# The first phase of an attention and maxout kernel written as one table, with the short group last and group 1 cut into a 4-tile chunk and three of 512 columns

## The chip, the cores and the metric

The kernel runs on one core of a Trainium2 chip. The metric is the time of one execution on the device in microseconds. The engines are named as in the profile: PE is the matrix engine (PEld its weight loads), DVE the vector engine, ACT the scalar engine, POOL the GpSimd engine, and SP (SyncE) the engine that issues nearly all transfers; SPq is SP's queue of transfer issues.

## The reference

For four batches of 12544 tokens with 128 channels, 32 inducing points first attend to all tokens, then every token attends to the 32 states that come out; each result goes through a maxout layer with an output projection.

```python
def mab(q, kv):
    s = scale * (q @ kv.transpose(0, 2, 1))
    s = s - s.max(-1, keepdims=True)
    a = np.exp(s)
    a /= a.sum(-1, keepdims=True) + 1e-09
    return a @ kv
h = mab(I, x)                       # 32 states for each batch
attn = mab(x, h)                    # tokens look at the states
y = np.maximum(np.maximum(attn @ w1, attn @ w2), attn @ w3) @ w_out
```

x is (4, 12544, 128); w1, w2 and w3 are (128, 768) and w_out is (768, 128). The weights arrive as 64-bit numbers.

## The kernel before

**Groups, chunks, slots.** The 98 tiles of 128 tokens of a batch form seven groups: group 0, the short one, has two tiles, groups 1 to 6 have sixteen. A full group makes four chunks of 512 columns, the short one a chunk of 256. A chunk is six slots, one for each 128 of the 768 hidden columns, so there are 600 slots in all. PE does two products for each slot (`pu`, L683, and `pv`, L689) out of the attention weights `pT` of the chunk and the batch's matrix `us` (states times weights, in a high and a low part). ACT takes the positive part of `pu` (L698), DVE the larger of both (`h`, L716), ACT makes the high part (`hi`, L705) and POOL, sometimes DVE, the low part (`lo`). `stage2` then adds three products for each slot into the chunk's output (L741 to L743, one more at its start, L740), six slots behind. `finish` copies the output and sends it off.

**First phase (batch 0).** Only batches 1 to 3 come with a transposed copy of x. For batch 0 PE transposes each group (`transpose_x`, L275) and ACT copies the result to `xT`. Then comes, group by group, the softmax of the 32 queries over the tokens: `attend_products` (PE, L285), `attend_max` (DVE), `attend_column` (ACT), `attend_spread` (PE, L309), `attend_least` (DVE), `attend_weights` (ACT), `attend_transpose` (DVE), `attend_sums` (PE, L360), `attend_keep` (ACT). The `combine_...` functions join the groups into the states `hT` (L528). Meanwhile the four weights are turned from 64 bits to float32 in the steps of `convert` (letters t, T, p, z, r, A or a, d, S), mostly on DVE. `transpose_w2` and `prep_products` form w2 times w_out, `prep_out` the high and low parts of w_out.

**From hT to the pipeline.** `scores_products` (PE, L599) and the ten steps of `scores_steps` give the token softmax of a group; its high and low part are `ph` and `pl`. For a full group `probs` copies four quarters of each chunk's rows into `pT` by transfers on SP (L668); the short group has its weights transposed on PE instead. `first_products` and `first_high`, `first_low` make `us`.

**What sets the order.** The schedule is manual: each engine runs its instructions in the order in which the program writes them, and SP issues its transfers in that order. `LOADS` orders the first loads (0 to 6 are groups, 7 w2, 8 w_out, 9 w1, 10 w3). `phase1_first` writes the first phase as a loop over the groups with the conversion steps of `WORK` in between; `ORDER` is a string for the stretch from hT to the pipeline, in which `d` puts two filler products on PE (`keep_busy`, L410). From then on `main` goes slot by slot: `advance` writes the products of the next slot, then come `probs` for the chunk two ahead (at the fifth slot of each chunk), `finish`, what `plan` holds for the slot, and `stage2`. `plan` spreads the scores of the next group and the first attention of the next batch (`softmax1`: maximum and `exchange_maxima`, six transfers on SP, L321, then `running_least` on DVE, L325) over the slots. The buffers that matter: five of `xg` (a group's tokens), one for the short group's, seven of `xT`, four of `pT`.

Of the kernel before, what the change touches and what calls it, by code (L numbers as in the profile page):

```python
# [25 lines left out]
def kernel(ctx, tc, x, xt, ind_t, w1, w2, w3, w_out, out):  # L26
# [4 lines left out]
    P = 128  # L31
# [7 lines left out]
    LOADS = (0, 1, 2, 7, 3, 8, 4, 5, 9, 6, 10)  # L39

    WORK = (
        "",
        ("0t 0T 0p 0z", "0r 0A"),
        ("1t 1T 1p 1z", "1r 1A"),
        ("0d 1d", "2t"),
        ("2T 2p 2z", "2r 2A"),
        ("3t 3T 3z", "3p 2d 2S"),
        "3r",
        "3a 3d 3S",
    )  # L50


    ORDER = "a a a a b a a b 0 c d m b a b a b a p d b 1 c s b b b s S m b q 2 c s 3 c s d s s d s"
# [70 lines left out]
    raws = []  # L124
    def first_loads():
        for what in LOADS:
            if what < NG:
                xg_next[(0, what)] = load_group(0, what, pieces=4 if what == 1 else 1)
            else:
                raws.append(load_raw(srcs[what - NG]))  # L130
# [79 lines left out]
    w2t = []  # L210

    def transpose_w2():
        for h in range(2):
            tpw = bank_v[h]
            for k in range(3):
                j = 3 * h + k
                nc.tensor.transpose(out=tpw[:, k * P : (k + 1) * P], in_=wf[:, 0, j * P : (j + 1) * P], identity=ident)
            w2h = hp.tile([P, 512], F32, name="w2h", tag="ru", bufs=3)
            nc.scalar.copy(out=w2h[:, : 3 * P], in_=tpw[:, : 3 * P])
            w2t.extend(w2h[:, k * P : (k + 1) * P] for k in range(3))  # L220

    def prep_products():

        wo = wf[:, 1, :].rearrange("p (j c) -> p j c", c=C)
        pw = bank_u[1]
        for j in range(NJ):
            nc.tensor.matmul(out=pw[:, :C], lhsT=w2t[j], rhs=wo[:, j, :], start=(j == 0), stop=(j == NJ - 1))

    def keep_products():
        nc.scalar.copy(out=wcat[:, 2 * DF :], in_=bank_u[1][:, :C])  # L230

    def prep_out():
        wo = wf[:, 1, :].rearrange("p (j c) -> p j c", c=C)
        nc.scalar.copy(out=wo_hi, in_=wo)
        nc.gpsimd.tensor_sub(out=wo_lo, in0=wo, in1=wo_hi.bitcast(F32))

# [3 lines left out]
    def start_batch(b):  # L240
        st = state[b] = {"xT": {}, "xg": {}, "a": {}, "s": {}}
# [28 lines left out]
    def transpose_x(b, gi, k):  # L270
        st = state[b]
        n = min(4, groups[gi]["nt"] - k)
        tps = (bank_u + bank_v)[k // 4]
        for i in range(n):
            nc.tensor.transpose(out=tps[:, i * P : (i + 1) * P], in_=st["xg"][gi][:, k + i, :], identity=ident)  # L275
        xv4 = st["xT"][gi].rearrange("p (q t l) -> p t q l", q=NQ, l=M)
        nc.scalar.copy(out=xv4[:, k : k + n, :, :], in_=tps[:, : n * P].rearrange("p (t q l) -> p t q l", q=NQ, l=M))  # L277
# [12 lines left out]
    def attend_max(b, gi):  # L290

        w = groups[gi]["nt"] * M
        st = state[b]
        mq = wk.tile([P, 1], F32, name="mq", tag="mq") if b == 0 else st["mx"][:, gi, 0:1]
        nc.vector.tensor_reduce(out=mq, in_=st["a"][gi][:, :w], axis=AX.X, op=ALU.max, negate=True)
        st["mq"] = mq

    def attend_column(b):

        st = state[b]  # L300
        md = wk.tile([P, NQ], F32, name="md", tag="md")
        nc.scalar.mul(out=md, in_=quad, mul=st["mq"])
        st["md"] = md

    def attend_spread(b, bank=None):

        st = state[b]
        st["mp"] = bank or spare[0]
        nc.tensor.matmul(out=st["mp"][:, :NQ], lhsT=sel, rhs=st["md"], start=True, stop=True)  # L309
# [102 lines left out]
    def phase1_first():  # L412

        start_batch(0)
        nc.sync.dma_start(out=iT, in_=ind_t)
        nc.scalar.mul(out=iT, in_=iT, mul=scale)
        first_loads()
        def half(gi, k):
            if gi < NG:
                if k == 0:  # L420
                    start_group(0, gi)
                for i in (k, k + 4):
                    transpose_x(0, gi, i)

        start_group(0, 0)
        keep_busy(6, bank_o[1])
        transpose_x(0, 0, 0)
        keep_busy(2, bank_o[1])
        attend_products(0, 0, bank_a[0])
        attend_max(0, 0)  # L430
        attend_column(0)
        half(1, 0)
        attend_spread(0, bank_o[0])
        attend_least(0, 0)
        half(1, 8)
        work(WORK[0])
        st = state[0]
        for gi in range(NG - 1):
            last = gi == NG - 2
            attend_products(0, gi + 1, bank_a[(gi + 1) % 2])  # L440
            attend_weights(0, gi)
            half(gi + 2, 0)
            attend_max(0, gi + 1)
            attend_column(0)
            half(gi + 2, 8)
            if gi > 0:
                attend_sums(0, gi - 1, bank_o[1])
                attend_keep(0, gi - 1)
            attend_transpose(0, gi)
            if not last:  # L450
                work(WORK[gi + 1][0])
            attend_spread(0, bank_o[0])
            attend_least(0, gi + 1)
            if gi == 3:
                transpose_w2()
            if last:
                prep_products()
            else:
                work(WORK[gi + 1][1])
        combine_least(st)  # L460
        work(WORK[NG - 1])
        combine_weights(st)
        attend_weights(0, NG - 1)
        keep_products()
        attend_sums(0, NG - 2, bank_o[1])
        attend_keep(0, NG - 2)
        combine_mask(st)
        combine_groups(st, range(NG - 1), bank_u[0])
        attend_transpose(0, NG - 1)
        sum_groups(st)  # L470
        attend_sums(0, NG - 1, bank_o[1])
        total_sums(st, bank_o[0])
        attend_keep(0, NG - 1)
        work(WORK[NG])
        invert_total(st)
        combine_groups(st, range(NG - 1, NG))
        combine_states(st, NQ)

# [19 lines left out]
    def combine_groups(st, which, bank=None):  # L498
        if which[0] == 0:
            st["sum"] = bank  # L500
        for gi in which:
# [4 lines left out]
                start=(gi == 0),  # L506
                stop=(gi == NG - 1),
# [28 lines left out]
    def first_products(st, which, bank):  # L536
        if which == 0:
            st["us"] = bp.tile([P, UW], F32R, name="us", tag="us")
            st["up"] = {}
# [3 lines left out]
        st["up"][which] = up, st["us"][:, cs]  # L543

# [456 lines left out]
```

## Time and profile before

| | us |
|---|---|
| median of 3 runs | 819.2 |
| lowest, highest | 818.54, 819.29 |
| the profiled execution | 818.58 |
| its span | 816.8 |
| PE busy in the span | 804.4 |
| ACT busy | 740.4 |
| POOL busy | 651.0 |
| DVE busy | 624.8 |

The span runs from the first to the last instruction; the execution's time has 1.8 us around it. Matmuls are pipelined, so PE's busy time says where it does nothing, and the distance from start to start says what a group of matmuls costs. In rows of the timeline come the start, the duration of the group, the engine, the line, the operation, what it writes and reads, the shapes, how many there are, and in brackets the idle time before and what ended it. A product in float32 shows as two records, a float32 transpose as one.

### The profile page before, as it was taken

The page shows a single profiled execution, that of the slowest core. Times are in us where ns is not written, and L with a number is a line of the kernel's source. Part 1 is how long each engine was busy: PE and PEld are TensorE (multiplying, and loading weights), DVE is VectorE, ACT ScalarE, POOL GpSimd, SP SyncE. Part 2 cuts the span into 40 slices and gives each one's busy share as a digit, 9 for nine tenths or more (in the row PEclk, how much of TensorE's full clock was granted, in tenths as well). Part 3 has the DMA queues.
Part 4 walks back from the last instruction along what each step waited for, and adds up shares of the span by engine and source line. Part 5 has one row for each costly group of instructions (what it writes and reads, how often), then busy time and mean ns, then how long its engine had stood idle before and what let it go on. Part 6 is the DMA issues. An engine that isn't in the chain of part 4 may idle for free.

```text
span 816.8 us, 14868 instructions
## 1 busy us (share of the span) xinstructions
PE 804.4 (98%) x4562; PEld 628.4 (77%) x4562; DVE 624.8 (76%) x1072; ACT 740.4 (91%) x1537; POOL 651.0 (80%) x521
## 2 busy tenths in 40 slices
PE   7989999999999999999999999999999999999998
PEld 5757778777788787777778777877878788787886
DVE  4978778777787687787786877877778788778874
ACT  5779889899899898898999988989889899899996
POOL 1369779878799798787888977977879889888887
PEclk9999999999999999999999999999999999999999
DMA  8843645263444453443534354523232222222221
GB/s 329 310 142 98 187 131 173 84 200 107 144 136 123 114 192 89 151 155 112 174 107 135 98 166 145 171 81 105 55 86 78 72 77 78 66 83 75 62 78 52
DMA packets 54287, 102.55 MB, mean 126 GB/s; under 512 B 19648, under 2 KB 23616, under 8 KB 48960
## 3 DMA queue, kind: packets, MB, share of 16 engines
q1 hardware_dynamic: 54064, 101.48, 39.4%
q8 instruction: 36, 0.59, 0.3%
q14 instruction: 43, 0.35, 0.1%
q10 hardware_dynamic: 144, 0.13, 0.0%
HBM read 48.12 MB, written 25.69 MB: 90 GB/s over the span
## 4 chain that ended last, share of the span: by engine, by line
PE 94%; DMA 3%; ACT 1%; DVE 1%; SPq 1%; issue 0%; DVEq 0%
PE acc L741 17%; PE pu L683 16%; PE pv L689 16%; PE acc L742 16%; PE acc L743 16%; PE aux L599 3%; PE acc L740 3%; PE acc L360 3%; PE aux L285 2%; DMA xg<-in_x_dram 2%; DMA pT<-pl 1%; ACT ru L698 0%; PE pu L275 0%; SPq L100 0%; ACT hi L705 0%; PE pv L275 0%
## 5 line engine op out<-in xcount | busy, mean ns | idle before, releaser
L713 POOL TENSOR_TENSOR lo<-h,hi 128x512 fp32r<-128x512 f32 (+1 forms) x502 | 635.8, 1298 | 124.9 <-ACT hi L705 83.1
L716 DVE TENSOR_TENSOR h<-pv,ru 128x512 f32<-128x512 f32 (+1 forms) x600 | 403.6, 675 | 165.1 <-PE pv L689 79.3
L698 ACT ACTIVATE ru<-pu 128x512 f32<-128x512 f32 (+1 forms) x600 | 376.2, 627 | 51.1 <-PE pu L683 48.0
L705 ACT CAST hi<-h 128x512 fp32r<-128x512 f32 (+1 forms) x600 | 387.2, 645 | 0.6 <-DVE h L716 0.3
L741 PE MATMUL acc<-hi,wo_hi 128*128 128x512 f32 (+1 forms) x600 | 235.1, 392 | 0.0
L683 PE MATMUL pu<-pT,us 128*128 128x512 f32 (+1 forms) x600 | 232.1, 387 | 0.5 <-DMA pT<-pl 0.4
L689 PE MATMUL pv<-pT,us 128*128 128x512 f32 (+1 forms) x600 | 232.0, 387 | 0.3 <-DVE h L716 0.3
L742 PE MATMUL acc<-hi,wo_lo 128*128 128x512 f32 (+1 forms) x600 | 231.3, 386 | 0.0
L743 PE MATMUL acc<-lo,wo_hi 128*128 128x512 f32 (+1 forms) x600 | 231.2, 385 | 0.0
L741 PEld LDWEIGHTS acc<-hi,wo_hi 128*128 128x128 f32 x600 | 112.6, 188 | 30.8 <-issue 8.7
L683 PEld LDWEIGHTS pu<-pT,us 128*128 128x128 f32 x600 | 112.6, 188 | 25.7 <-ACT ru L698 2.0
L689 PEld LDWEIGHTS pv<-pT,us 128*128 128x128 f32 x600 | 112.6, 188 | 23.8 <-DVE h L716 1.6
L743 PEld LDWEIGHTS acc<-lo,wo_hi 128*128 128x128 f32 x600 | 112.7, 188 | 23.1
L742 PEld LDWEIGHTS acc<-hi,wo_lo 128*128 128x128 f32 x600 | 112.7, 188 | 21.8
L719 DVE TENSOR_TENSOR lo<-h,hi 128x512 fp32r<-128x512 f32 x98 | 70.9, 724 | 1.5 <-ACT hi L705 1.5
L758 ACT COPY o<-acc 128x512 f32<-128x512 f32 (+1 forms) x99 | 61.2, 618 | 0.0
L740 PE MATMUL acc<-pT,us 128*128 128x512 f32 (+1 forms) x100 | 38.8, 388 | 0.0
L360 PEld LDWEIGHTS acc<-xg,aT 128*32 128x32 f32 x768 | 21.1, 110 | 11.3 <-issue 6.9
L285 PE MATMUL aux<-xT,iT 128*32 128x512 f32 x192 | 25.3, 598 | 1.6 <-ACT xT L277 1.6
L360 PE MATMUL acc<-xg,aT 128*32 128x128 f32 x768 | 25.6, 274 | 0.0
L599 PE MATMUL aux<-xT,hT 128*32 128x512 f32 x192 | 25.1, 603 | 0.0
L192 POOL TENSOR_TENSOR rest<-rest,t 128x768 f32<-128x768 f32 x3 | 5.5, 1827 | 23.9 <-DVE rest L184 23.9
(121 smaller groups left out, 422.0 us busy)
## 6 DMA issues: line engine op xcount, KB each, us to landing
out_dram<-o SPq DMA_DIRECT2D x95, 256.0 KB, 2.1
xg<-in_x_dram SPq DMA_DIRECT2D x23, 1024.0 KB, 6.1
xT<-in_xt_dram SPq DMA_DIRECT2D x18, 1024.0 KB, 5.6
pT<-ph SPq DMA_DIRECT2D x192, 64.0 KB, 2.0
pT<-pl SPq DMA_DIRECT2D x192, 64.0 KB, 2.0
raw<-in_w_dram SPq DMA_DIRECT2D x3, 768.0 KB, 8.9
us<-uh SPq DMA_DIRECT2D x24, 52.0 KB, 1.9
us<-ul SPq DMA_DIRECT2D x24, 52.0 KB, 1.9
```

What stands on the lines that cost most here:

```text
L360: nc.tensor.matmul(out=hps[q * M : (q + 1) * M, :C], lhsT=aT[:, t * M : (t + 1) * M], rhs=xg[:, t, :], start=(t < NQ), stop=(t + NQ >= nt),)
L683: nc.tensor.matmul(out=pu[:, :w], lhsT=state[c.b]["us"][:, 2 * j * P : (2 * j + 1) * P], rhs=c.pT[:, :w], start=True, stop=True)
L689: nc.tensor.matmul(out=pv[:, : d.w], lhsT=state[d.b]["us"][:, (2 * j + 1) * P : (2 * j + 2) * P], rhs=d.pT[:, : d.w], start=True, stop=True,)
L698: nc.scalar.activation(out=ru[:, :w], in_=pu[:, :w], func=AF.Relu)
L705: nc.scalar.copy(out=hi[:, : c.w], in_=h[:, : c.w])
L713: nc.gpsimd.tensor_sub(**args)
L716: nc.vector.tensor_max(out=h[:, : d.w], in0=pv[:, : d.w], in1=relus.pop(s)[:, : d.w])
L719: nc.vector.tensor_sub(**low)
L740: nc.tensor.matmul(out=c.acc[:, :w], lhsT=us[:, 2 * DF :], rhs=c.pT[:, :w], start=True, stop=False)
L741: nc.tensor.matmul(out=c.acc[:, :w], lhsT=wo_hi[:, j, :], rhs=c.hh[j][:, :w], start=False, stop=False)
L742: nc.tensor.matmul(out=c.acc[:, :w], lhsT=wo_lo[:, j, :], rhs=c.hh[j][:, :w], start=False, stop=False)
L743: nc.tensor.matmul(out=c.acc[:, :w], lhsT=wo_hi[:, j, :], rhs=c.hl[j][:, :w], start=False, stop=(j == NJ - 1))
```

## The change

- One table, `FIRST`, is the order of everything from the start to slot 12; `WORK`, `ORDER` and `phase1_first` are gone. A letter is a function and the digits are its arguments (T transposes, C copies, P products, M maximum, D, R, N, E, X, S, K the further steps of the first attention; B and Q filler products; U, h, l, g, H the making of `us`; y `probs` of a chunk; z `stage2`).
- `LOADS` begins with groups 1, 2 and 3, the short group and w_out come last; group 1 comes in two pieces instead of four; `iT` is loaded on ACT's queue. The groups are joined in the order of `TURN`.
- The fillers are seven at the start (before six and two) and 19 single ones (before four pairs).
- Group 1 of batch 0 is cut into a chunk of its first four tiles (`HEAD`), whose weights are transposed on PE, and three chunks of 512 columns over the other twelve tiles, whose rows are 384 columns long (`pieces`). Its softmax runs as two (steps `a` and `b`).
- The scores of group 2 move from the head to slot 12; batch 1's group 0 moves: its maximum from slot 10 to 13, `running_least` from slot 16 to 18, the next load of tokens from slot 7 to 13. `stage2` runs four slots behind until slot 13, then six.
- `prep_products` and the rest of w_out move behind hT; the addition of w3 goes from DVE to POOL; of chunk 1, slots 1 and 4 have their low parts on DVE.

```diff
-    LOADS = (0, 1, 2, 7, 3, 8, 4, 5, 9, 6, 10)
...
+    LOADS = (1, 2, 3, 7, 4, 9, 5, 10, 6, 0, 8)
+    TURN = (1, 2, 3, 4, 5, 6, 0)
+    HEAD = 4
+    LOWHEAD = (1, 4)
+    FIRST = (
+        "B7 T11 T10 T13 C11 T12 C10 C13 C12 P1 M1 D1 T22 C22 T23 T21 R1 T20 C23 N1 E1 X1 T33 T32 C20 T30 C21 "
+        "C33 0t 0T T31 0z 0p S1 0r C30 C31 P2 C32 K1 T41 P3 C41 M2 M3 D2 0A B1 R2 T42 N2 2t D3 R3 T43 E2 T40 "
+        "C42 B1 C43 B1 T52 0d 2T T51 N3 T53 C40 C52 X2 C51 2p T50 C53 P4 C50 3t S2 2r E3 P5 3z B1 3T T60 3p "
+        "M4 T63 2z K2 D4 C60 B1 R4 M5 X3 T61 N4 D5 C63 3r T62 T00 1t R5 C61 E4 W1 C62 N5 2A B1 1T S3 X4 E5 "
+        "C00 P6 K3 P0 X5 M6 S4 1z B1 D6 M0 R6 2d n2 B1 K4 N6 3A D0 B1 R0 1p S5 E6 N0 W0 E0 cl X6 K5 S6 2S cw "
+        "X0 lw lt K6 cm w1 S0 3d K0 1r cg123456 3S cg0 iv B1 hT B1 qS sT qA qB aT U1 w0 sm U0 am sx se bT 1A "
+        "sr ax ae g1 si bm sp bx h1 B1 h0 su sh 1d be sl ar B1 Oh br U2 ai l0 ap bi js bp h2 Gp au ks g2 bu "
+        "H1 Ol H2 Gk s0 ah Q1 s1 bt U3 al n3 4h s2 Q1 Q1 bh Q1 Q1 s3 ja ka 4l bl y2 s4 y3 Q1 s5 z0 s6 z1 s7 "
+        "z2 s8 z3 z4 s9 z5 s10 y4 s11 z6 s12 z7 "
     )
-    ORDER = "a a a a b a a b 0 c d m b a b a b a p d b 1 c s b b b s S m b q 2 c s 3 c s d s s d s"
+    STEPS1 = (7, 8, 9, 10, 11, 11, 12, 13, 14, 15)
     STEPS2 = (3, 5, 7, 8, 9, 10, 11, 13, 14, 15)
...
-                xg_next[(0, what)] = load_group(0, what, pieces=4 if what == 1 else 1)
+                xg_next[(0, what)] = load_group(0, what, pieces=2 if what == LOADS[0] else 1)
...
-        nc.sync.dma_start(out=iT, in_=ind_t)
+        nc.scalar.dma_start(out=iT, in_=ind_t)
...
+    def probs(c):
+
         if c.q is None:
+            probs_transposes(c, bank_a[1])
+            probs_keep(c, nc.vector.tensor_copy)
+            return
+        src = state[c.b]["p", c.gi, c.first]
+        c.pT = pT = wk.tile([P, 512], F32R, name="pT", tag="pT", bufs=4)
+        for r in (0, 2, 1, 3):
+            for q, at, n, to in c.pieces:
+                nc.sync.dma_start(
+                    out=pT.bitcast(F32)[r * M : (r + 1) * M, to : to + n], in_=src[r % 2][q * M : (q + 1) * M, at : at + n]
                 )
...
+    def pieces(k):
+
+        row = (GT - HEAD) * M
+        ends = sorted({512 * k, 512 * k + 512} | {q * row for q in range(NQ) if 0 < q * row - 512 * k < 512})
+        return [(a // row, a % row, b - a, a - 512 * k) for a, b in zip(ends, ends[1:])]
...
+            kinds = [(None,)]
+            if groups[gi]["nt"] == GT:
+                kinds = [(q,) for q in range(NQ)]
+                if b == 0 and gi == 1:
+                    kinds = [(None, HEAD)] + [(k + 1, None, pieces(k)) for k in range(NQ - 1)]
...
-                elif b > 0 or g > 1:
+                else:
                     first.append((scores_products, b, g + 1, bank_a[0]))
-                softmax2(b, g + 1, *(s0 + i for i in STEPS2))
+                softmax2(b, g + 1, *(s0 + i for i in (STEPS2 if b > 0 or g > 1 else STEPS1)))
...
-                        at(s0 + 1, load_tokens, 1, 4)
+                        at(s0 + 7, load_tokens, 1, 4)
...
-                    softmax1(n, 0, s0 + 2)
+                    softmax1(n, 0, *((s0 + 2,) if b > 0 else (s0 + 5, -1)))
...
-            burst(s0 + 2, *first)
+            burst(s0 + 2 if b > 0 or g > 1 else s0 + 6, *first)
...
-            if s >= LAG:
-                c, j = slots[s - LAG]
-                stage2(c, j)
-                if j == NJ - 1:
-                    over = c
+            if done[0] <= s - (LAG if s >= begins[0] + 8 else LAG - 2):
+                over = second()
...
+            "B": lambda n: keep_busy(n, bank_u[1]),
+            "Q": lambda n: keep_busy(n, bank_o[0]),
...
+            "qS": lambda: scores_products(0, 0, bank_u[0]),
+            "qA": lambda: scores_products(0, 1, bank_a[0], 0, HEAD),
+            "qB": lambda: scores_products(0, 1, bank_a[1], HEAD),
+            "js": lambda: probs_transposes(first, bank_u[1]),
+            "ks": lambda: probs_keep(first, nc.scalar.copy),
+            "ja": lambda: probs_transposes(head, bank_a[0]),
+            "ka": lambda: probs_keep(head, nc.scalar.copy),
+            "n2": lambda: (start_batch(1), load_channels(1, 0)),
+            "n3": lambda: load_channels(1, 1),
```

In the table, lower-case pairs that begin with s, a or b are steps of the softmax of the short group, of the head and of the twelve other tiles (`bh` and `bl` are the high and low part of the last, `ph` and `pl`), s with a number is an `advance`, z with a number a `stage2`.

More of the change, by code (lines that the diff above doesn't have):

```diff
@@ L268, in load_channels, with transpose_x, keep_x @@
         state[b]["xg"][gi] = xg_next.pop((b, gi))
[L270 to L277, printed above, removed]
+    def transpose_x(gi, i):
+        st = state[0]
+        if gi not in st["xT"]:
+            start_group(0, gi)
+        tps = (bank_u + bank_v)[i]
+        for k in range(min(4, groups[gi]["nt"])):
+            nc.tensor.transpose(out=tps[:, k * P : (k + 1) * P], in_=st["xg"][gi][:, 4 * i + k, :], identity=ident)
+    def keep_x(gi, i):
+        n = min(4, groups[gi]["nt"])
+        tps = (bank_u + bank_v)[i]
+        xv4 = state[0]["xT"][gi].rearrange("p (q t l) -> p t q l", q=NQ, l=M)
+        nc.scalar.copy(
+            out=xv4[:, 4 * i : 4 * i + n, :, :], in_=tps[:, : n * P].rearrange("p (t q l) -> p t q l", q=NQ, l=M)
+        )
     def attend_products(b, gi, bank):
@@ L410, in keep_busy, with begin @@
             nc.tensor.matmul(out=bank[:, 2 * P : 3 * P], lhsT=ident, rhs=ident, start=True, stop=True)
-    def phase1_first():
+    def begin():
         start_batch(0)
-        nc.sync.dma_start(out=iT, in_=ind_t)
+        nc.scalar.dma_start(out=iT, in_=ind_t)
         nc.scalar.mul(out=iT, in_=iT, mul=scale)
         first_loads()
[L418 to L477, printed above, removed]
     def combine_least(st):
@@ L745, in finish @@
     def finish(c):
[L746 removed]
+        g = groups[c.gi]
+        at = g["at"] + (c.q or 0) * c.w
         o = op.tile([P, 512], F32, name="o", tag="o", bufs=3)
+        if c.q is None and c.last < g["nt"]:
+            nc.scalar.copy(
+                out=o.rearrange("p (q t l) -> p t q l", q=NQ, l=M), in_=c.acc.rearrange("p (t q l) -> p t q l", q=NQ, l=M)
+            )
+            nc.sync.dma_start(
+                out=out[c.b, :, at : at + g["nt"] * P].rearrange("p (q n) -> p q n", q=NQ)[:, :, : c.w // NQ],
+                in_=o.rearrange("p (q n) -> p q n", q=NQ),
+            )
+            return
+        if c.first:
+            nc.scalar.copy(out=o, in_=c.acc)
+            for q, col, n, to in c.pieces:
+                col += g["at"] + (q * g["nt"] + HEAD) * M
+                nc.sync.dma_start(out=out[c.b, :, col : col + n], in_=o[:, to : to + n])
+            return
         if c.n == len(chunks) - 1:
@@ L779 @@
     plan = [[] for _ in range(len(slots) + LAG)]
-    per_batch = nch * NJ
-    short = NJ if groups[0]["nt"] < GT else 0
+    begins = [min(c.n for c in chunks if c.b == b and c.gi == 1) * NJ for b in range(B)]
     WIN = NQ * NJ
@@ L881, with second, main @@
                         at(s0 + 18, load_channels, n + 1, 1)
-            burst(s0 + 2, *first)
+            burst(s0 + 2 if b > 0 or g > 1 else s0 + 6, *first)
             burst(s0 + 15, *second)
-    def main():
-        over = None
-        for s in range(len(slots) + LAG + 1):
+    done = [0]
+    def second():
+        c, j = slots[done[0]]
+        done[0] += 1
+        stage2(c, j)
+        return c if j == NJ - 1 else None
+    def main(start, over):
+        for s in range(start, len(slots) + LAG + 1):
             if s >= LAG:
@@ new lines @@
+        for step in FIRST.split():
+            kind, rest = step[0], step[1:]
+            if step in names:
+                names[step]()
+            elif kind in steps and not rest.isdigit():
+                next(steps[kind])
+            elif kind == "c":
+                combine_groups(st, [int(g) for g in rest[1:]], bank_u[0])
+            elif kind.isdigit():
+                convert(int(kind), rest)
+            elif kind == "s":
+                advance()
+            elif kind == "z":
+                if over:
+                    finish(over)
+                over = second()
+            elif kind == "f":
+                finish(over)
+                over = None
+            elif kind == "y":
+                probs(tails[rest])
+            else:
+                one[kind](*[int(v) for v in rest])
@@ L947 @@
+        for gen in steps.values():
+            assert next(gen, None) is None
+        main(pipe["next"], over)
 _GT = 16
```

270 lines of the change are left out of this document (138 added, 132 removed).

## The prediction

> **What bounds the kernel now.** The page first: TensorE is busy 98% of the span, and the granted clock reads full everywhere. Then the busy time by stages, which says where the missing 2% lie.
>
> ```profile
> PE 804.4 (98%) x4562; PEld 628.4 (77%) x4562; DVE 624.8 (76%) x1072; ACT 740.4 (91%) x1537; POOL 651.0 (80%) x521
> PEclk9999999999999999999999999999999999999999
> ```
> ```profile
> 1.30:20.20 18.90, 14.74 (x108) 10.40 (x108) 8.69 (x20) 11.25 (x25) 2.34 (x3) 1.00 0.94 352
> 20.20:41.90 21.70, 20.41 (x306) 15.73 (x306) 19.53 (x34) 15.39 (x39) 7.35 (x5) 1.00 0.79 296
> 41.90:53.90 12.00, 10.17 (x62) 5.53 (x62) 9.67 (x24) 8.02 (x21) 6.46 (x7) 1.00 0.35 114
> 53.90:71.00 17.10, 17.10 (x90) 13.94 (x90) 14.23 (x26) 16.54 (x37) 15.88 (x14) 1.00 0.58 177
> 71.00:800.00 729.00, 728.89 (x3942) 572.28 (x3941) 564.79 (x958) 678.50 (x1397) 607.54 (x482) 1.00 0.38 116
> ```
>
> The columns after the window are its length and then the busy time of PE, weight loads, DVE, ACT and POOL. From 53.9 us on PE stands still for 0.1 us in 746. So whatever the change does to the time shows as an earlier or later arrival at one given PE instruction of the full pipeline, with the same work done by then. I use the `pv` product of slot 21 (at 70.91, below): before it, both kernels have run the first phase, all weight products, the scores of group 2, the attention product of batch 1's group 0 and the output products of slots 0 to 14. In the first 53.9 us PE idles 4.2 + 1.3 + 1.8 us plus 1.3 us of start, and runs 16 filler products (the first eight below, in 16 records; the others by four `d` of ORDER).
>
> ```profile
> 1.37 2.93 PE L410 MATMUL acc<-ident 128*128 128x128 f32 x12 [1.37 <-POOL ident masks.py:199]
> ...
> 4.51 0.65 PE L410 MATMUL acc<-ident 128*128 128x128 f32 x4
> ...
> 20.24 1.09 PE L275 MATMUL pu<-ident,xg 128*128 128x128 f32 x8 [0.73 <-DMA xg<-in_x_dram]
> 21.17 1.04 PE L275 MATMUL pv<-ident,xg 128*128 128x128 f32 x8
> 22.13 1.08 PE L360 MATMUL acc<-xg,aT 128*32 128x128 f32 x32
> 23.14 0.39 PE L309 MATMUL acc<-md,sel 128*128 128x4 f32 x2
> 23.46 1.06 PE L285 MATMUL aux<-xT,iT 128*32 128x512 f32 x8
> 24.46 1.09 PE L275 MATMUL pu<-ident,xg 128*128 128x128 f32 x8
> ...
> 37.97 1.55 PE L502 MATMUL pu<-sw,hg 128*128 128x64 f32 x12
> 39.45 1.08 PE L360 MATMUL acc<-xg,aT 128*32 128x128 f32 x32
> ...
> 53.86 0.50 PE L683 MATMUL pu<-pT,us 128*128 128x512 f32 x1 [0.38 <-DMA pT<-pl]
> ...
> 70.91 0.40 PE L689 MATMUL pv<-pT,us 128*128 128x512 f32 x1
> ```
>
> Starts minus starts give a group's price on PE: 16 transposes 1.89, sums 1.01, spread 0.32, attention product 1.00, together 4.2 us.
>
> **Part 1: order of loads (gain).** Loads go one behind the other, 1024 KB a group, 768 KB a weight.
>
> ```profile
> 12.93 0.56 DVE L171 TENSOR_SCALAR t<-raw 128x768 uint32<-128x768 uint32 x1 [1.67 <-DMA raw<-in_w_dram]
> ...
> 17.76 0.64 DVE L171 TENSOR_SCALAR t<-raw 128x768 uint32<-128x768 uint32 x1 [0.47 <-DMA raw<-in_w_out_dram]
> ...
> 41.59 0.29 DVE L528 TENSOR_TENSOR hT<-pu,rec 128x128 f32<-128x128 f32 x1
> ```
> ```profile
> 12.93:39.94 27.01, 24.30 (x332) 17.61 (x334) 25.28 (x42) 20.32 (x50) 7.79 (x5) 1.00 0.90 344
> ```
> ```profile
> L196 DVE SCALAR_TENSOR_TENSOR wf<-size,rest 128x768 f32<-128x768 f32 x2 | 2.5, 1298 | 0.0
> L192 DVE TENSOR_TENSOR rest<-rest,t 128x768 f32<-128x768 f32 x1 | 0.9, 949 | 0.0
> ```
>
> Before, w2 lands at 12.93 as KB 2960 of the stream (16 + 128 + 1024 + 1024 + 768) and w_out at 17.76 as KB 4752: 371 KB per us. After, w2 is KB 3840, on this line 15.3, and group 4 is KB 4864, 18.1 (before 5776 and 20.24). The first group no longer stands behind `iT` (now on ACT's queue) and the short group, which is up to 0.9 us, and it comes in two pieces instead of four: bounds for w2 13.6 to 15.3, for group 4 16.3 to 18.1. I take 14.2 and 16.8.
>
> **Part 2: the first phase up to hT (gain 2.7).** From group 4's first transpose PE still has 12 transposes of four (5.6), four products (4.0), six spreads (1.9), five sums (5.05), the w2 transposes (0.8), the combination (1.5 + 0.7) and the short group's own (0.6): 20.1 us. Ten single fillers lie in this stretch, 0.65/2 = 0.33 each by the 4.51 row (two products, four records), so 0 to 3.3 us. DVE: 25.28 us busy from w2 to its last step; after, the addition of w3 (0.95, to POOL) and one of the two long `wf` steps (1.3) leave the stretch, group 1's maximum, least and transpose (1.5) move ahead of it and the short group's (0.6) into it: 22.2 plus the last reciprocal and product, 0.9. PE alone ends at 36.9 to 40.2, DVE at 37.3 plus what it waits for PE, about 1 to 1.5. Both are nearly full, so they delay each other; I take 39.2 for the end of hT (bounds 37.1 and 41.2) against 41.88. The six `w_out` products (1.5) are no longer in it; they go where PE waits after hT.
>
> **The fillers.** The first 12 products took 2.93 us, the later 4 took 0.65: PE starts at half pace and is at full pace from about 4.1 us on, through waits of up to 0.8 us. A filler thus buys nothing by the trace; its price is 0 (in a pause) to 0.33. The Trainium skill, "TensorE: Matmul & The Clock Gate", Part 1, says that the clock falls back only after an idle window of about 3.4 us; no PE wait here is that long, so by it too the 19 fillers cannot shorten anything, and a case in which they do gets no chance.
>
> **Part 3: hT to group 1's `ph` (loss of 1.9 of it).** ACT sets this stretch in both.
>
> ```profile
> 40.76 0.84 ACT L234 CAST wo_hi<-wf 128x768 fp32r<-128x768 f32 x1
> ...
> 47.80 0.59 ACT L547 CAST us<-acc 128x512 fp32r<-128x512 f32 x1
> ...
> 49.01 0.38 ACT L698 ACTIVATE ru<-pu 128x256 f32<-128x256 f32 x1
> 49.29 0.58 ACT L645 CAST ph<-aux 128x512 fp32r<-128x512 f32 x1
> ```
>
> Before, `ph` is done at 49.87, 8.0 us after hT. After, the exponentials of the short group and of the 4-tile head come first (DVE has eight steps of 0.1 to 0.5 before them: hT + 3.0). Then ACT has, before `bh` ends: five 512-column copies (0.5 to 0.6, 2.75), `wo_hi` 0.84, the 384-column exponential and `bh` itself (0.46 each), five small ones (0.25), three relus and one cast of 256 columns (0.28): 6.9. So `bh` ends at hT + 9.9 = 49.1, where the head's route over PE is not involved. The head itself reaches its first `pu` (slot 6) at about hT + 11.4 = 50.6 against 53.86: four more transposes (0.5) replace the DMA wait, and there the change is 3.3 us ahead, 2.8 when the moved scores of group 2 (+1.0) and one output step already done (-0.5) are counted.
>
> **Part 4: SyncE's queue (gives the gain back).**
>
> ```profile
> 49.89 1.23 SPq L668 DMA_DIRECT2D pT<-ph  x2
> ...
> 60.17 3.72 SPq L321 DMA_DIRECT2D mx<-mx  x6
> 63.99 0.53 SPq L759 DMA_DIRECT2D out_dram<-o  x1
> 64.56 0.43 SPq L111 DMA_DIRECT2D xT<-in_xt_dram  x1
> ...
> 70.00 0.35 SPq L759 DMA_DIRECT2D out_dram<-o  x1
> ...
> 97.08 0.38 SPq L111 DMA_DIRECT2D xT<-in_xt_dram  x1
> ```
> ```profile
> DMA to landing us min/median/max: 1.7/1.7/2.8
> ```
> ```profile
> 66.20 0.15 DVE L325 TENSOR_REDUCE mx<-mx 128x1 f32<-128x4 f32 x1
> 66.66 0.69 DVE L716 TENSOR_TENSOR h<-pv,ru 128x512 f32<-128x512 f32 x1 [0.32 <-PE pv L689]
> ```
>
> The three 512-column chunks each cross a boundary of the 384-column rows, so `pieces` gives two parts and each chunk 8 transfers: 24, all issued (`y2`, `y3`, `y4`) ahead of slot 13, where `exchange_maxima` of batch 1 issues six more. Before, only eight stood ahead of it. At 0.61 each (1.23/2; the tiny exchange ones cost 0.62 too, so size does not matter) they take 14.6 us from 49.1: 63.8. Then the output of chunk 0 (0.53), `load_tokens` (0.43), gaps 0.1: the exchange starts at 64.9, its last issue at 68.0, and lands 1.7 later, 69.7. `running_least` stands on DVE at slot 18, which PE reaches about 64.5; everything behind it, the maxima of slots 19 on too, waits some 5 us. PE runs on until `pv` of slot 21, which needs `h` of slot 19: 69.7 + 0.15 + 0.69 = 70.6. Without this wait PE would be there at 68.1. Before: 70.91. The loads of batch 1's groups 1 to 3 now wait in the same queue behind the short group's buffer, until about 37 instead of 27; they and `xT` (4 MB) are through by 49, so I cost them at nothing; if not, `y2` lands late.
>
> **Sum.** Profiled execution 818.58 (span 816.8 + 1.8), its median 819.2: -0.3 gives 818.9. The bound for a narrow transfer's issue is 0.35 to 0.62 (the row of 70.00, among the shortest on this queue, and the row used); I take the row of the same line.
>
> **Rivals.** (a) Faster: the exchange is not last, because narrow pieces issue at 0.35 (24 in 8.4 us, done by 57.5, ahead of slot 13) or DVE's wait is taken up by the buffers: then the 2.8 us stay, 816.4. For: the head is ready sooner. Against: the 0.62 of the tiny exchange. (b) Slower: the exchange lands behind the 1 MB load issued just before it.
>
> ```profile
> 98.77 5.38 DMA pT<-pl
> ```
> ```profile
> xT<-in_xt_dram SPq DMA_DIRECT2D x1, 1024.0 KB, 4.6
> ```
>
> A small transfer issued at 98.77 behind the load of 97.08 took 5.38 instead of 1.7. Counted from the load's issue (7.1 on 64.4) that is 71.5, from its own 73.4: slot 21 at 72.3 to 74.2, +1.4 to +3.3, 821.6 in the middle. It decides if the exchange takes over 3.5 us to land. Against: alone, 1 MB landed in 4.6, 69.0 here, before the 69.7. The Trainium skill, "DMA: Bandwidth & Descriptors", "Queues, rings and completion order", has each DMA engine take its descriptors in ring order, which is this rival; by it alone the sum is 820.6. The trace agrees at 98.77. (c) The first phase does not end earlier (hT at 41.2, fillers in full): everything is 2.0 later, 820.9.
>
> **Numbers.** Forecast, the gain is spent on the exchange: 0.43 (own range 817.6 to 820.8, from hT +-1.3). (a) 0.30, plus 0.04 for an hT below 37.9: faster 0.34. (b) 0.17, (c) 0.06: slower 0.23. A measurement of this kernel tells 0.2%, 1.6 us. Low 815.6 is (a) with hT 0.8 earlier, high 822.0 cuts the end of (b).
>
> **What would show it.** Right: w2's first step on DVE at 13.6 to 15.3; hT ending near 39.2; slot 6 near 50.6; 24 `pT` issues in one row of about 14.6 us; `running_least` waiting for a DMA some 5 us, and PE idle 2 to 3 us near 68. Wrong: an issue time well under 0.6 for pieces, no DVE wait there, or PE short of work elsewhere after 54 (a late `y2` at slot 12).

## The result and the profile after

The change made the kernel slower: 825.9 us at the median (825.5 to 827.6) against 819.2, a ratio of 1.0091 (95% interval 1.0078 to 1.0105). The forecast was 818.9 with 815.6 to 822.0, so the time lies outside the range, on the side to which rival (b) pointed, and beyond its 821.6. The profiled execution took 825.47 with a span of 823.7.

The page of the changed kernel, busy time of TensorE with its instruction count, and the granted clock:

```profile
PE 809.5 (98%) x4594; PEld 632.1 (77%) x4594; DVE 626.9 (76%) x1081; ACT 741.2 (90%) x1540; POOL 652.1 (79%) x520
PEclk9999999999999999999999999999999999999999
```

That page still reads 98% for TensorE and a full clock. The stages say more (length, then busy time of PE, weight loads, DVE, ACT, POOL, then granted clock, DMA share and GB/s):

```profile
1.30:20.20 18.90, 17.71 (x144) 13.55 (x145) 8.43 (x17) 11.96 (x26) 1.83 (x2) 1.00 0.98 394
20.20:41.90 21.70, 19.08 (x296) 14.90 (x298) 19.46 (x35) 13.79 (x37) 9.35 (x6) 1.00 0.35 120
41.90:53.90 12.00, 11.42 (x86) 8.48 (x75) 10.84 (x34) 10.09 (x29) 9.05 (x8) 1.00 0.85 349
53.90:71.00 17.10, 16.88 (x87) 11.99 (x85) 13.01 (x22) 15.74 (x33) 14.56 (x14) 1.00 0.34 104
71.00:90.00 19.00, 14.55 (x63) 10.44 (x64) 11.05 (x20) 12.91 (x27) 10.75 (x10) 0.91 0.37 106
```

Up to 53.9 PE is busier than before (48.2 against 45.3 us), fillers included. The loss stands in the last row: 4.45 us of idle PE where before there was none, and a clock of 0.91. The timelines of PE, DVE and SyncE's queue show what it is (start, length, then the instruction; in brackets the idle time before it and what ended it):

```profile
50.34 0.48 ACT L599 CAST ph<-aux 128x384 fp32r<-128x384 f32 x1
```
```profile
50.85 2.77 SPq L631 DMA_DIRECT2D pT<-ph  x4
...
63.80 2.50 SPq L631 DMA_DIRECT2D pT<-pl  x4
66.40 0.53 SPq L744 DMA_DIRECT2D out_dram<-o  x1
66.97 0.43 SPq L101 DMA_DIRECT2D xg<-in_x_dram  x1
67.50 3.73 SPq L328 DMA_DIRECT2D mx<-mx  x6
```
```profile
68.80 0.70 DVE L584 TENSOR_TENSOR aux<-aux,rsr 128x512 f32<-128x512 f32 x1
74.57 0.16 DVE L332 TENSOR_REDUCE mx<-mx 128x1 f32<-128x4 f32 x1 [5.07 <-DMA mx<-mx]
```
```profile
51.82 0.36 PE L707 MATMUL acc<-pT,us 128*128 128x256 f32 x1
...
52.37 0.43 PE L645 MATMUL pu<-pT,us 128*128 128x512 f32 x1
...
70.41 0.48 PE L645 MATMUL pu<-pT,us 128*128 128x512 f32 x1
75.45 0.76 PE L651 MATMUL pv<-pT,us 128*128 128x512 f32 x1 [4.57 <-DVE h L678]
76.14 1.94 PE L293 MATMUL aux<-xT,iT 128*32 128x512 f32 x8
...
82.19 0.39 PE L707 MATMUL acc<-pT,us 128*128 128x512 f32 x1
```

Four rows of before for the same places; the `aux` row is the eight attention products of one part of a group:

```profile
54.78 0.28 PE L740 MATMUL acc<-pT,us 128*128 128x256 f32 x1
...
70.67 0.40 PE L683 MATMUL pu<-pT,us 128*128 128x512 f32 x1
...
71.24 1.06 PE L285 MATMUL aux<-xT,iT 128*32 128x512 f32 x8
75.99 0.39 PE L740 MATMUL acc<-pT,us 128*128 128x512 f32 x1
```

The output products of chunk 0 start 3.0 earlier than before (51.82 against 54.78) and those of chunk 2 only 0.3 (67.21 against 67.50), as the scores of group 2, two more slots and some 0.9 us of small delays now stand between the two. The product directly ahead of the `pv` of slot 21, a `pu`, starts 0.26 earlier than before (70.41 against 70.67): that is the whole lead when the wait begins. The `pv` of slot 21 starts 4.5 later (75.45 against 70.91), chunk 3's output 6.2 later (82.19 against 75.99), the last chunk's 6.9 (815.52 against 808.65). So a small lead turns into a loss at one wait, and 1.7 more are lost right behind it, where nothing waits. The second loss is the clock. The windows of the changed kernel, one microsecond each:

```profile
75.00:76.00 1.00, 0.55 (x1) 0.25 (x1) 1.00 (x3) 1.00 (x4) 0.00 (x0) 0.76 0.97 401
76.00:77.00 1.00, 1.00 (x6) 0.21 (x9) 1.00 (x4) 1.00 (x3) 0.76 (x1) 0.50 0.95 318
...
78.00:79.00 1.00, 1.00 (x10) 0.55 (x5) 0.00 (x0) 0.00 (x0) 1.00 (x1) 0.54 0.44 107
```

After the pause the granted clock is 0.50 for 3.4 us, and the eight products take 1.94 instead of 1.06. The forty slices of the page, 20 us each, are too coarse to show it.

### The profile page after: what moved, and what is told of

Its sections match the earlier page's. It is cut to its first block, busy times and chain, and to the rows that moved or that the text cites. A ratio compares the mean times of both kernels' runs of the same rounds, so it can differ in the third digit from the quotient of the medians.

```text
span 823.7 us, 15143 instructions
## 1 busy us (share of the span) xinstructions
PE 809.5 (98%) x4594; PEld 632.1 (77%) x4594; DVE 626.9 (76%) x1081; ACT 741.2 (90%) x1540; POOL 652.1 (79%) x520
## 4 chain that ended last, share of the span: by engine, by line
PE 91%; DMA 4%; DVE 2%; ACT 1%; issue 1%; SPq 0%; DVEq 0%; ACTq 0%
PE acc L708 17%; PE pv L651 16%; PE pu L645 16%; PE acc L709 16%; PE acc L710 16%; PE aux L548 3%; PE acc L707 3%; PE acc L367 2%; PE aux L293 2%; DMA raw<-in_w_dram 2%; DMA pT<-ph 1%; DMA iT<-in_ind_t_dram 1%; DMA mx<-mx 0%; ACT ru L660 0%; ACT hi L667 0%
## 5 line engine op out<-in xcount | busy, mean ns | idle before, releaser
L743 ACT COPY o<-acc 128x512 f32<-128x512 f32 (+1 forms) x95 | 58.4, 614 | 0.0
L193 POOL TENSOR_TENSOR rest<-rest,t 128x768 f32<-128x768 f32 x4 | 8.1, 2031 | 24.4 <-DVE rest L185 24.4
L548 PE MATMUL aux<-xT,hT 128*32 128x512 f32 (+2 forms) x200 | 25.1, 586 | 0.0
```

## The experiments

The theory before the first run: SyncE's queue puts the exchange of batch 1's maxima behind 24 narrow transfers, DVE stands at that exchange, PE at DVE, and PE's clock falls in the pause. The rivals: the load of 1 MB ahead of the exchange makes it late; the clock alone is the loss; the time that DVE lost in two steps of the weight conversion beside POOL moves everything. e1 to e4 and e9 are the changed kernel with one edit, e5 with two; the others put edits together. Medians in us, ratios to the kernel before on the same chip:

| kernel | median | ratio (95%) | chunk 0 / chunk 3 / last chunk, start of output |
|---|---|---|---|
| before | 819.2 | | 54.78 / 75.99 / 808.65 |
| changed | 825.9 | 1.0091 (1.0078 to 1.0105) | 51.82 / 82.19 / 815.52 |
| e1: chunk 4's transfers behind the exchange | 821.8 | 1.0028 (1.0017 to 1.0038) | 52.14 / 77.83 / 811.43 |
| e2: load behind the exchange | 824.8 | 1.0068 (1.0053 to 1.0083) | 51.82 / 81.39 / 815.61 |
| e3: 16 products in the pause | 825.4 | 1.0075 (1.0060 to 1.0091) | 51.61 / 81.05 / 814.81 |
| e4: POOL's additions placed later | 824.7 | 1.0063 (1.0048 to 1.0078) | 49.36 / 80.25 / 813.74 |
| e5: half of chunk 4's transfers behind | 821.4 | 1.0023 (1.0012 to 1.0034) | 51.75 / 77.22 / 811.41 |
| e6: e4 and e5 | 820.0 | 1.0006 (0.9994 to 1.0018) | 49.45 / 74.72 / 809.18 |
| e7: e6 without the 19 fillers | 817.9 | 0.9975 (0.9963 to 0.9987) | 49.11 / 74.13 / 808.79 |
| e8: e7, two loads later | 817.3 | 0.9978 (0.9966 to 0.9989) | 49.14 / 73.87 / 807.21 |
| e9: changed, without the 19 fillers | 825.0 | 1.0072 (1.0050 to 1.0093) | 51.66 / 82.96 / 816.22 |
| e10: e8 with the 19 fillers | 819.5 | 0.9999 (0.9990 to 1.0009) | 49.55 / 75.34 / 810.40 |
| e11: e8 again | 816.7 | 0.9968 (0.9956 to 0.9980) | 48.86 / 73.28 / 806.17 |

**e1: the exchange ahead of chunk 4's transfers.**

```
-        "z2 s8 z3 z4 s9 z5 s10 y4 s11 z6 s12 z7 "
+        "z2 s8 z3 z4 s9 z5 s10 s11 z6 s12 z7 "
```

> The changed kernel with the third chunk's eight transfers (y4) no longer written ahead of slot 11 but where the planner puts them, at slot 16, behind the exchange. Theory 1 (the exchange is late because 24 transfers stand ahead of it on SyncE): with 16 ahead it starts when its maximum is ready, about 63.9 us instead of 67.5, lands near 69.5, DVE waits under 1 us for it instead of 5.1, PE's pause of 4.6 us and the half clock of 3 us behind it (1.7 us) go: 819 +- 1 us. Rival A (the exchange is late because the transfers of the same six descriptors land slowly, 4 to 6 us after issue behind a 1 MB load, wherever they are issued): DVE still waits 2 to 4 us: 822 to 824. Rival B (y4 is now late for slot 24): a new PE wait of 1 to 3 us near 76 us: 821 to 822.

SyncE's queue in e1:

```profile
64.20 3.73 SPq L328 DMA_DIRECT2D mx<-mx  x6
...
68.61 3.16 SPq L631 DMA_DIRECT2D pT<-ph  x4
71.81 2.59 SPq L631 DMA_DIRECT2D pT<-pl  x4
```

The exchange starts 3.3 us earlier (64.20 against 67.50), DVE's wait for it and the fall of the clock are gone, and 4.1 of the 6.7 us come back. What is left is a new wait of PE, 1.3 us, at the first product of chunk 4; the trace names ACT as its releaser, which had long been done, while the last transfer of chunk 4 is issued only at about 74. The `pv` of slot 21 starts at 71.07, level with before (70.91) and not ahead of it. So the queue is the cause of the long wait, and rival B of the expectation came true beside theory 1: eight transfers too many on either side of the exchange cost something.

**e2: the load behind the exchange.**

```
-                        at(s0 + 7, load_tokens, 1, 4)
+                        at(s0 + 8, load_tokens, 1, 4)
```

> The changed kernel with the 1 MB load of batch 1's group 4 issued at slot 14 instead of 13, so behind the exchange on the same queue and not ahead of it. Theory 1 with the ring order (the small transfers landed 3.8 to 6.1 us after issue because they lie behind 1 MB): they land 1.7 us after issue, the last near 72 instead of 74.4, PE's pause shrinks from 4.6 to about 2 us, which leaves the clock up: 821.3, or 823 if the clock still falls. Rival (the landing has nothing to do with the load): only the 0.47 us of the issue are won: 825.

The exchange starts at 67.46, as it did. Two rows from the chain of waits of e2, and for comparison the landing of the last transfer in the changed kernel (start, length and what):

```profile
68.70 1.89 SPq L328
...
71.91 1.76 DMA mx<-mx
```
```profile
70.64 3.75 DMA mx<-mx
```

The last transfer now lands after 1.76 us instead of 3.75, but one of the six issues took 1.89 instead of 0.6, and all six 5.04 instead of 3.73. PE still waits 3.6 us (4.6 with the load ahead), and the clock falls all the same. The load ahead of the exchange is worth 0.9 us of the pause; the medians are 1.0 apart, with intervals that overlap. So the load is at most a part of the cause.

**e3: keep PE busy in the pause.**

```
+                        at(s0 + 14, lambda: keep_busy(16, spare[0]))
```

> The changed kernel with 16 more filler products (about 4 us at full pace) on PE at slot 20, just before the pause; the wait for the exchange stays as it is. If the half clock of 75.8 to 78.9 us costs 1.7 us of its own, and comes from the pause: the granted clock stays at 1.00 there and the time is 823.8. Rival (the slow products at 76 to 79 us are slow for another reason, such as the transfers landing then): 825.5, and if the fillers push PE's own work back: up to 829.

The windows of e3 from 74 to 80 in one row:

```profile
74.00:80.00 6.00, 5.00 (x28) 2.86 (x27) 4.04 (x8) 4.17 (x11) 2.78 (x3) 1.00 0.83 251
```

The clock stays at 1.00, so the fall comes from the pause. From the `pv` of slot 21 to chunk 3's output PE needs 5.27 us (75.78 to 81.05) instead of 6.74, with 5.08 before; chunk 3's output starts 1.1 us earlier than in the changed kernel. But by chunk 12 only 0.2 us of that is left, the medians differ by 0.4 us and the intervals overlap. The clock's fall is a consequence of the wait that costs about 1.5 us where it happens; that it costs as much at the end is not shown, and alone it doesn't explain the loss.

**e4: two POOL additions one step later.** In the table, `2r` goes to the place ahead of `M4` and `3r` to the place ahead of `X4`.

```
-   ... S2 2r E3 ... 3p M4 ... C63 3r T62 ... S3 X4 E5
+   ... S2 E3 ... 3p 2r M4 ... C63 T62 ... S3 3r X4 E5
```

> The changed kernel with two steps of the weight conversion moved on DVE: 2r from before 3T to just before M4, 3r from before 1t to just before X4, so that POOL's additions 2A and 3A start later, while DVE runs maxima out of PSUM and transposes and not the steps 2p and 1T, which took 2.07 and 2.48 us beside POOL instead of 0.56 and 0.96. Theory 2 (DVE stands still in these two steps until POOL's addition ends, and that is the 2.4 us by which hT came later than predicted): both steps take their 0.56 and 0.96 again, hT ends near 39 instead of 41.5, group 1's ph, the 24 transfers and the exchange move with it, the wait stays: 823.3. Rival (PE with its fillers sets hT): hT moves by under 1 us: 825.

First the changed kernel, DVE and POOL side by side, and then e4:

```profile
25.06 2.07 DVE L181 TENSOR_SCALAR pw<-t 128x768 uint32<-128x768 uint32 x1
30.36 2.48 DVE L176 SCALAR_TENSOR_TENSOR t<-raw,t 128x768 uint32<-128x768 uint32 x1
...
41.24 0.29 DVE L474 TENSOR_TENSOR hT<-pu,rec 128x128 f32<-128x128 f32 x1 [0.58 <-PE pu L448]
```
```profile
24.31 2.41 POOL L193 TENSOR_TENSOR rest<-rest,t 128x768 f32<-128x768 f32 x1 [6.19 <-DVE rest L185]
29.93 2.09 POOL L193 TENSOR_TENSOR rest<-rest,t 128x768 f32<-128x768 f32 x1 [3.22 <-DVE rest L185]
```
```profile
24.25 0.56 DVE L181 TENSOR_SCALAR pw<-t 128x768 uint32<-128x768 uint32 x1
28.57 0.95 DVE L176 SCALAR_TENSOR_TENSOR t<-raw,t 128x768 uint32<-128x768 uint32 x1
...
38.79 0.29 DVE L474 TENSOR_TENSOR hT<-pu,rec 128x128 f32<-128x128 f32 x1 [0.58 <-PE pu L448]
```
```profile
25.75 1.82 POOL L193 TENSOR_TENSOR rest<-rest,t 128x768 f32<-128x768 f32 x1 [8.13 <-DVE rest L185]
30.47 1.83 POOL L193 TENSOR_TENSOR rest<-rest,t 128x768 f32<-128x768 f32 x1 [2.90 <-DVE rest L185]
```

Two DVE steps of 0.56 and 0.95 (`3p`, which the expectation calls 2p, and `1T`) took 2.07 and 2.48, ending 0.4 and 0.8 after POOL's additions. With the additions elsewhere both are short again and `hT` ends at 39.08, 2.45 earlier. The Trainium skill, "SBUF — State Buffer", says that VectorE and GpSimd share a pair of ports, and that of two instructions that both need it the first holds it to its end while the other stands. The rows of DVE agree: its two steps start after POOL's additions and end just behind them. That the additions are longer too, 2.41 and 2.09 against 1.82, goes beyond that sentence. Later expectations call the moved steps score steps; they are steps of the weight conversion. Of the 2.45 us only 1.2 reach the median: the exchange moves along with the first phase (DVE still waits 5.1 and PE 4.6), and the clock is at half for 6.8 us in the windows, twice as long.

**e5: chunk 4's transfers in two halves.** The four of the high part stay in front, the four of the low part go behind the exchange, and two loads of batch 1 go to slot 18.

```
-        "... s10 y4 s11 ..."
+        "... s10 v4 s11 ..."
...
+            elif kind == "v":
+                probs(tails[rest], (0, 2))
...
-                        at(s0 + 7, load_tokens, 1, 4)
-                    at(s0 + 9, load_channels, n, 2)
+                        at(s0 + 8, lambda: probs(chunks[4], (1, 3)))
+                        at(s0 + 12, load_tokens, 1, 4)
+                    at(s0 + (9 if b > 0 else 12), load_channels, n, 2)
```

> The changed kernel with SyncE's queue reordered: of the third chunk's eight transfers the four of the high part stay where y4 stands, the four of the low part come at slot 14 behind the exchange; the two 1 MB loads of slots 13 and 15 (tokens of group 4, channels of group 2 of batch 1) come at slot 18, behind all of them. Theory 1 (order on SyncE's queue alone costs the 6 us): the exchange starts near 64, lands near 69.5, the last of the eight lands near 70.5 and slot 24 is not late (in e1 it was, by 1.3 us or more): no wait of DVE for the exchange, no PE pause over 0.5 us after 54 us: 819 to 819.5, what the changed kernel would be without the queue. Rival (PE, ACT and POOL after slot 12 are set by something else in the new head, such as stage2 four slots behind): still 820.5 or more.

The exchange is issued from 64.61 to 68.34; DVE waits 1.7 and PE 1.2 us for it, and no window is under 1.00. 821.4 is as much as e1, and the rival's figure, not the 819 to 819.5 of theory 1: a better order on the queue gives 4.5 of the 6.7 us back. Of the rest, a part is again the wait for the exchange.

**e6: e4 and e5 together.**

> e5 and e4 together: SyncE's queue reordered and 2r and 3r moved on DVE. If the 2.4 us that e4 won at hT were only lost to the wait for the exchange, which moved with it, they show now: e5 minus 2.4, 816.5 to 817. Rival (the pipeline after slot 12 takes them back, since ACT and POOL are full there): within 1 us of e5.

820.0: with e4's edit e5 is 1.4 us faster, though the intervals overlap, and level with the kernel before; the expectation had 2.4, or under 1. The exchange is issued from 62.30 on, DVE waits 1.4 for it and PE 0.9.

**e7: e6 without the 19 single fillers** (all `B1` and `Q1` taken out of the table).

> e6 without the 19 single filler products (the seven at the start stay). If they lie in PE's pauses and the clock does not need them (no pause there is over 1.3 us): the same as e6 within 0.4 us. If they push PE's work back (0.33 each, ten of them before hT): up to 1.5 us less than e6. If the clock falls without them (PE's pauses grow to over 3 us): 1 to 3 us more, with a granted clock under 1.00.

817.9, 2.1 us less than e6 where at most 1.5 was expected, and 0.25% faster than the kernel before. From the chain of waits of e7, start, length and what:

```profile
72.85 7.93 DMA pT<-pl
...
80.87 0.47 PE pu L647
```

A narrow transfer of chunk 5 needs 7.93 us, issued 2 us behind the two loads that e5 had moved to slot 18; PE waits 1.1 for it.

**e8: e7, with those two loads at slot 23.**

```
-                        at(s0 + 12, load_tokens, 1, 4)
-                    at(s0 + (9 if b > 0 else 12), load_channels, n, 2)
+                        at(s0 + 17, load_tokens, 1, 4)
+                    at(s0 + (9 if b > 0 else 17), load_channels, n, 2)
```

> This is the kernel of the run without fillers (score steps of group 4 and 6 reordered, the exchange between the two halves of chunk 4's transfers, no single fillers), with the two batch-1 loads of slot 18 moved to slot 23, behind the transfers that chunk 5 needs. In the run without fillers the chain of waits shows one of those transfers, `pT<-pl`, landing 7.93 us after its issue, behind the loads, and TensorE waiting 1.1 us for it at 79.7. Theory A (that wait is what is left of the queue's cost): the transfer lands about 2 us after issue, the wait goes, chunk 5's output starts 1.1 to 1.4 us earlier, and the median falls from 817.9 to 816.5 to 816.9 (the lowest single runs without fillers, 816.4 and 816.7, are those in which the load happened to be out of the way). Theory B (the kernel has slack again by chunk 13, where that run stood level with before; the wait costs nothing at the end): 817.5 to 818.3. Theory C: the 1 MB of tokens and the columns now come late for batch 1 and a new wait of TensorE or VectorE for them appears: over 818.5.

SyncE's queue in e8:

```profile
70.58 1.15 SPq L633 DMA_DIRECT2D pT<-ph  x2
71.82 1.17 SPq L633 DMA_DIRECT2D pT<-pl  x2
73.04 0.57 SPq L101 DMA_DIRECT2D xg<-in_x_dram  x1
73.71 0.40 SPq L112 DMA_DIRECT2D xT<-in_xt_dram  x1
```

The wait is gone, and in the trace the last chunk starts 1.6 us earlier; the ratio, 0.9978, is not to be told from e7's 0.9975. The profiled execution of e7 was among its slowest; that the wait cost less in the others is likely, but not shown.

**e9: the changed kernel, only the fillers out.**

> The changed kernel with the 19 single fillers left out of its first phase and nothing else changed: exchange, transfers and the order of the score steps stay. In the pair of runs with the reordered steps and the split transfers, leaving them out was worth 2.1 us at the median. Theory A (fillers stand in the path of the first phase and everything behind it, the exchange included, moves up with them): 825.9 - 2.1 = 823.2 to 824.3. Theory B (fillers keep the clock up in the pauses; without them the clock falls somewhere in the first phase): a window under 1.00 before 60 us and 826 or more. Theory C (what sets the end here is the exchange behind 24 transfers, and the transfers start when `ph` of the four-tile chunk is there, which the fillers don't move by more than 0.4 us): 825.2 to 826.0.

825.0, beside 825.9 with intervals that overlap. `hT` ends where it did (41.26 start against 41.24), so the fillers were hidden there, behind DVE and POOL; the exchange starts at 68.34, PE waits 3.6 us and the clock falls. As long as the exchange sets the end, taking out fillers brings at most 0.8 us.

**e10 and e11: the best kernel with the fillers back in, and without them once more**, side by side on one chip.

> The fastest kernel so far (score steps reordered, exchange between the halves of chunk 4's transfers, loads at slot 23, no single fillers; 817.3) with the 19 single fillers put back, so that their price is told without a transfer waiting behind a load. Taking them out of the changed kernel alone moved it from 825.9 to 825.0, intervals touching; taking them out of the kernel with reordered steps and split transfers moved it from 820.0 to 817.9. Theory A (they stand in PE's path, some 2 us): ratio to the kernel before 1.0000 to 1.0010, and slots 6 and 21 some 0.3 to 1 us later than without them. Theory B (their price in the first phase is the 0.3 us by which the first chunk's output moved, and the rest of the 2.1 us was the wait behind the load, which fell differently): ratio 0.9978 to 0.9986. Theory C (they are worth something, since they keep the granted clock up in the first phase): ratio below 0.9970.

> The fastest kernel again, without fillers, on the same chip as the run with them, so that the two stand beside each other: 817 to 818, ratio 0.997 to 0.999.

819.5 against 816.7, ratios 0.9999 and 0.9968 with separate intervals: the 19 fillers cost 2.8 us here, as theory A has it, and 2.1 between e6 and e7. A part is seen: `hT` is 0.5 us later with them, the first output product 0.7 (49.55 against 48.86), and the exchange half a us later:

```profile
69.23 0.16 DVE L332 TENSOR_REDUCE mx<-mx 128x1 f32<-128x4 f32 x1 [1.98 <-DMA mx<-mx]
```
```profile
67.08 0.16 DVE L332 TENSOR_REDUCE mx<-mx 128x1 f32<-128x4 f32 x1 [0.24 <-DMA mx<-mx]
```

The first row is e10, the second e11. The last issue starts at 65.6 and 65.2; the landing follows 3.6 us later in one and 1.9 in the other, and PE waits 1.5 us in e10 and nothing in e11: 2.1 at chunk 3. That the landing differs for the fillers' sake is not shown. By the last chunk the two traces, of one of the slowest executions of e10 and of the fastest of e11, are 4.2 apart, of which 1.2 came between 295 and 345 us and 0.9 after that. That stretch takes 0.4 to 1.3 us more than before in the changed kernel and in the seven others with fillers, and nothing more in the four without them; no fillers run there, and in the changed kernel no wait of PE is over 0.2 us and none of its weight loads over 0.6. Why stays open.

**A coincidence in all runs.** The traces list 36 or 37 transfers of 16 KB of the kind "instruction" on the DMA queue q8. One of them starts beside the exchange in the changed kernel (at 71.2), e2 and e3 (68.7), e4 and e6 (66.1), e5 (68.4) and e10 (66.9), and just behind it in e1 (69.0). Where it starts while the exchange is being issued (e2, e3, e4), one issue takes 1.9 to 2.2 us instead of 0.6. Where it starts after the last issue (changed, e5, e6, e10), that last transfer lands after 3.0 to 3.75 us, in e5, e6 and e10 with no load ahead. In e7, e8, e9 and e11 none starts during the exchange, and it is issued in 3.73; its last transfer lands within 1.9 us, and after 2.5 in e9, which has the load ahead. No run moves this transfer alone, so it is a rival for the part of the landing that the load does not explain, and not a shown cause.

The kernel of e8 and e11 is the fastest here: 0.9978 and 0.9968 of the kernel before.

## Why the prediction was wrong, step by step

The forecast named the wait that sets the time, but three of its terms were too small: `hT` (39.2, measured 41.5), the landing of the exchange (1.7, measured 3.9) and the clock after the pause (nothing, measured 1.7). The first also took most of the lead that was to pay for the wait.

**Part 1, right, and earlier than its bounds.** w2's first step was at 13.11 (bound 13.6), and group 4's first transposes at 15.92 (bound 16.3; I took 16.8):

```profile
13.11 0.52 DVE L172 TENSOR_SCALAR t<-raw 128x768 uint32<-128x768 uint32 x1
```
```profile
15.92 0.66 PE L277 MATMUL pu<-ident,xg 128*128 128x128 f32 x4
```

**Part 2, a term mis-sized: `hT` at 41.5 instead of 39.2.** The sum took w3's addition, which the change moved to POOL, off DVE (0.95), and counted POOL's additions as free for DVE. In the trace two of them, w1's and w3's, took 3.04 us of DVE's time in its own steps (1.51 and 1.53 over the 0.56 and 0.95). e4 shows what `hT` is without that: 39.08. That it comes so near to 39.2 is in part luck, since 39.2 was picked between 37.1 and 41.2. The upper bound, 41.2, was 0.3 too low.

**The fillers, right at the wrong end.** "0 to 0.33 each" is 0 to 6.3 us for 19; I said that they could not shorten anything, which e9, e10 and e11 bear out, but let only the first ten into the sum. They cost 2.1 to 2.8 us where they are in the path, and at most 0.8 in the changed kernel, where the exchange hides them.

**Part 3, right by its own count.** `ph` of group 1 ends at `hT` + 9.3 (50.82 less 41.53; predicted 9.9), and slot 6 starts at `hT` + 10.8 (52.37; predicted 11.4). With Part 2's error slot 6 is 1.5 us ahead of before and not 3.3, and by slot 21 only 0.26 is left (70.41 against 70.67), where the prediction had 2.8 without the wait. So even an exchange in time would have left the kernel level with before there, as e1 does (71.07 against 70.91).

**Part 4, the mechanism right, the sum not.** The 24 transfers stand in one row of 15.45 us (50.85 to 66.30; predicted 14.6), DVE waits 5.07 for the exchange ("some 5 us"), and PE stands at the `pv` of slot 21, the product named. One count was wrong: before, not eight but twelve transfers stand ahead of the exchange (49.89 to 58.67 on SyncE's queue, which then idles until 60.17); the sum doesn't use it. The time is off by three terms, two here and the clock below. The exchange starts at 67.50 instead of 64.9: 2.6, of which 2.3 is `hT`. DVE's maximum starts 3.9 after its last issue (70.64 to 74.57) instead of the 1.7 taken from the median landing, +2.2. The condition of rival (b), over 3.5 us, was met. From the issues' side the trace gives

```profile
xg<-in_x_dram SPq DMA_DIRECT2D x1, 1024.0 KB, 6.5
...
mx<-mx SPq DMA_DIRECT2D x2, 0.1 KB, 5.0
```

but e2, with that load behind, shows that at most about 1 us of it is the load ahead, which was rival (b)'s reason. In e5, e6 and e10, with no load ahead, DVE's maximum still starts 3.1 to 3.6 after the last issue; for the rest there is only the coincidence with q8 named above, and its cause stays open. The Trainium skill, "DMA: Bandwidth & Descriptors", "Queues, rings and completion order", has each DMA engine take its descriptors in ring order, and the 7.93 us of e7 behind two loads agree with it. Together the two terms are 4.85 us at slot 21: 75.45 for 70.6.

**The step that was missing: the clock.** I excluded it because no PE wait of before was long, and then predicted a new wait of 2 to 3 us without asking the same of that. It became 4.6 us and cost 1.7 in the trace (4.54 late at slot 21, 6.20 at chunk 3), 1.5 of which e3 took away there, though not at the end. Last, 0.7 more between 300 us and the end, whose cause stays open. 4.85 + 1.7 + 0.7 = 7.2 on the 818.3 that the sum gave on the profiled execution's scale is 825.5, the profiled time.

The comparison with rival (c), `hT` at 41.2, 820.9, was right in its place and right in its size for the first phase; it was given 0.06 since it was taken for an alternative to the late exchange. Both happened, and since the exchange starts when `ph` is there, their terms add.

## What to carry to other kernels

When an edit makes one transfer into several narrow ones, count the issues on the queue up to the next small transfer that an engine in the path waits for: here 24 issues of 0.6 us, 12 more than before, made the wait, and moving eight of them, or four and two loads, gave 4.1 to 4.5 of 6.7 us back. Price a landing by its range and not by the median: the engine that waited for the same transfer went on 1.8 to 3.9 us after its issue. If the forecast has a new wait of TensorE, add what the clock does after it, and ask of every operation on another engine which short steps of the first one will stand beside it, and what they took there.

## What the hardware showed

- VectorE steps of 0.56 and 0.95 us beside a GpSimd addition took 2.07 and 2.48, and the addition 2.41 and 2.09 instead of 1.82; with the additions beside other steps (e4) all were short.
- The clock can fall early in a pause. In e4 PE stands still from 68.55 and the windows are

```profile
70.00:71.00 1.00, 0.00 (x0) 0.00 (x0) 0.00 (x0) 0.00 (x0) 0.00 (x0) 0.76 0.11 17
...
77.00:78.00 1.00, 1.00 (x5) 0.78 (x5) 0.00 (x0) 0.06 (x1) 0.00 (x0) 0.83 0.43 105
```

  so it fell about 2 us into the pause and rose 6.8 us later; in the changed kernel PE stands still from 70.89, the clock fell about 4.6 us later and stayed down 3.4 us. In e2 and e9 it fell 3.8 and 2.8 us into the pause, for 3.3 and 6.8 us. The Trainium skill, "TensorE: Matmul & The Clock Gate", Part 1, has windows of about 3.4 us that run by themselves; the two lengths, one and two such windows, agree, while a fall after 2 us is earlier than the idle window of 3.4 us that I had taken from it as a condition. Pauses of 0.9 to 1.5 us, in e1, e5, e6 and e10, lowered nothing.
- Six exchange transfers of a few hundred bytes take 3.73 us to issue, 0.62 each, in the changed kernel and eight other runs, and 5.04 to 5.33 in e2, e3 and e4; four pieces of 16 to 48 KB take 2.42 to 2.50 in every row of the changed kernel but the first, which is no more for each. DVE's maximum starts between 1.8 (e2) and 3.9 us after the last one is issued, where it waits for it.
